# A decode kernel of two layers: 640 columns of ring given to resident W_q, another fill order for the first MLP's ring, no unread products in the first and last norm

## The chip, the cores and the metric

The kernel runs on one core of one Trainium2 chip. The metric is the device time of one execution in microseconds (us). Several executions of each kernel are timed and the median is taken; one more execution is profiled, and every duration below comes from that one.

## The reference

Two layers run one after the other on a single token of each of four sequences (B = 4, D = 640). Both layers use the same weights and the same caches. A layer is an attention over the last 1024 positions of a cache of 32 heads of 128, and then a gated MLP of width 1728; both are added to the residual, and both read a layernorm without weights.

```python
def _A_ref(x, k_cache, v_cache, wq, wo):
    W = min(4096, max(256, Sk // 4))          # 1024
    q = (x @ wq).reshape(B, Sq, Hq, Dh)       # 32 heads of 128, then transposed
    k, v = k_cache[:, :, Sk - W:, :], v_cache[:, :, Sk - W:, :]
    scores = jnp.einsum("bhqd,bhkd->bhqk", q, k) * (Dh ** -0.5)
    p = _softmax(scores, axis=-1)
    o = jnp.einsum("bhqk,bhkd->bhqd", p, v)
    return o.transpose(0, 2, 1, 3).reshape(B, Sq, Hq * Dh) @ wo

def _B_ref(x, W_gate, W_up, W_down):
    gate, up = x @ W_gate, x @ W_up
    return (gate * (gate > 0) * up) @ W_down

x = x + _A_ref(_layernorm(x), ...)
x = x + _B_ref(_layernorm(x), ...)
x = x + _A_ref(_layernorm(x), ...)
x = x + _B_ref(_layernorm(x), ...)
```

Everything is float32. Both layers need all of K and V of the 1024 positions, W_q, W_o and the MLP; they are loaded twice, but for the part that stays on the chip.

## The kernel before

The host lays out all weights and caches as four long arrays of 128 rows, in the order in which the kernel uses them: `heads` (W_q, K, W_o and V of heads 0 to 26, in six groups of four and one of three), `kept` (the same for heads 27 to 31, in groups of three and two), `mlp`, and `limbs` (the last 512 columns of V of head 17, cut into short pieces for a few rows). The two kept groups are K0 and K1 (KEPT = 5 heads): the first layer uses them last, the second layer first, and they stay in memory between.

**The store.** One tile, `store`, of 128 rows x STORE floats holds all that is loaded. A second, `first_q`, of HELD floats keeps the first columns of `heads` (W_q of the first group and a part of the second's) for both layers. HELD + STORE is constant. A list `plan` names every load in order: its array, its columns, and the place in `store` that it is written to. `put` adds loads to it, `stretch` adds a long run of them that goes round `store` as a ring (pieces of at most MOST floats, three to a lap, LAP).

**What sets the order.** `load()` issues loads from the plan on SP, strictly in order, until one whose place still holds data that is to be used (`live`). Each use of data ends in `done`, which frees the columns that were used and calls `load()` again. So each load is issued behind the instruction that uses its place for the last time, and a load that can't be issued holds up all that come after it in the plan. SP does nothing else. This order is fixed when the program is built; on the chip, SP waits on TensorE's semaphore.

**TensorE's order in attention**, for a group g with the group `before` and the group `after`: totals and transposed probabilities of g, `query` of the group after next, `scores(after)` (uses K of the next group), `project(before)` (uses W_o of the group before), `values(g)` (uses V of g). In the first layer the part of `heads` that is used last is thus W_q ..., V of heads 20 to 23, W_o of heads 20 to 23, V of heads 24 to 26, W_o of heads 24 to 26.

**From the heads to the kept part.** In the first layer, `kept` is loaded while the last heads are still being used. The columns of `heads` from `turn` on lie in `store` from 2 * KEPT * D = 6400; `turn` is the first cut (an end of a part that can be used by itself) from which all the rest fits in. Over them `kept` is written in pieces: 6400 to 18688, 18688 to 26880, 26880 to 33536, and five more. The third one's end is written as v0 + 6656.

**The first MLP.** Then 47360 floats (FRONT) of `store` are taken by `kept`. The MLP of the first layer goes through a small ring: the space above FRONT, and three places inside the kept part, AHEAD (768 floats, named `a` in the plan), AWAY (`q`, 1280) and BACK (`k`, 1728), whose data ScalarE copies to `probs` and to PSUM for that time. AWAY's data comes back after down(0). The lists `gu`, `gu_end` and `wd` give the places and sizes of the MLP's loads by hand. `gate(j)` uses the columns of a quarter of W_gate and W_up, in pieces of 256 floats; `down(j)` uses W_down in four pieces of 640, in the order down(3), down(0), down(1), down(2). Behind the MLP's loads come the first loads of the second layer's `heads`, from column HELD on, into the same ring, then a ring that grows as the kept data is used.

**Unread products.** `busy` and `fill` multiply the identity with itself into PSUM, where nobody reads it, when `waits[0]` is set. `normalized` sets it and issues two transposes and one product.

Of the kernel before, what the change touches and what calls it, by code (L numbers as in the profile page):

```python
# [57 lines left out]

HELD = 4288
STORE = 50624
FRONT = KEPT * 2 * (D + KV)


# [1 line left out]
BACK = FRONT - 2 * KV - 1728, FRONT - 2 * KV  # L67
AWAY = BACK[0] - 1280, BACK[0]
HOME = 12864
FIRST, MOST = 32384, 16192  # L70
LAP = 3 * MOST
SPLIT, PART = 17, 2048
LIMBS = [(half + i, 5, 0, 1536) for i in range(4) for half in (0, 32)] + [(i, 2, 1536, PART) for i in range(4)]
# [39 lines left out]
def decode_kernel(ctx: ExitStack, tc: tile.TileContext, x, source, out):  # L113
# [21 lines left out]
    def put(layer, row, to, *cuts):  # L135

        for lo, hi in zip(cuts, cuts[1:]):
            assert 0 < hi - lo <= MOST and to % 64 == 0 and lo % 32 == hi % 32 == 0 and to + hi - lo <= STORE, (row, lo, hi, to)
            plan.append((layer, row, lo, hi, to))
            to += -(-(hi - lo) // 64) * 64  # L140
        return to
# [29 lines left out]
    q_end = 2 * KEPT * D  # L171
    turn = min(c for c in ROWS["heads"][2] if c >= heads_end - (STORE - q_end))
    mid = [near(turn + (heads_end - turn) * i // 3) for i in (1, 2)]
    to = stretch(0, HELD, turn, FIRST)
    assert to <= KEPT * D or to > 2 * MOST, to
    put(0, "kept", KEPT * D, KEPT * D, q_end)
    put(0, "heads", q_end, turn, *mid, heads_end)
# [2 lines left out]


    f, z, a, q, k = FRONT, STORE - D, AHEAD[0], AWAY[0], BACK[0]
    assert STORE - FRONT == 2 * 1280 + 64 + D
    gu = [(z, D), (f, 1280), (f + 1280, 1344), (a, 768), (k, 960), (k + 960, 768), (q, 1280)]
    gu_end = [(f, 1280), (f + 1280, 1280), (f + 2560, D)]
    wd = [(a, D), (k, 960), (k + 960, D), (q, 1280), *gu_end, (a, D), (k, D), (k + D, D)]
    lo = 0
    for to, n in gu + gu + gu_end + wd:
        put(0, "mlp", to, lo, lo + n)
# [2 lines left out]


    lo = HELD
    for to, n in (f, 1280), (f + 1280, 1280), (f + 2560, D + 64), (a, 768), (k, 1728):
        put(1, "heads", to, lo, lo + n)
        lo += n
    to = AHEAD[1]
# [10 lines left out]
    to = put(1, "heads", to, lo, hi)  # L209
    lo, hi = hi, near(hi + STORE - to)  # L210
    put(1, "heads", to, lo, hi)
    last = near(heads_end - 25216)
    to = stretch(1, hi, last, 0)
    for lo, hi in (last, near(last + 12800)), (near(last + 12800), heads_end):
        to = put(1, "heads", to if to + hi - lo <= STORE else 0, lo, hi)
    cuts = [0, 7040, 12160, GU0 + 3 * GU, WD1 + WD, MLP - 4 * D, MLP - 2 * D, MLP - D, MLP - QUARTER, MLP]
    for lo, hi in zip(cuts, cuts[1:]):
# [152 lines left out]
            nc.tensor.matmul(m[32 * g:32 * g + 32], sel_q, a, start=True, stop=True, tile_position=(0, 32 * g))  # L370
        return m

    def normalized():

        ysb, xc, sq = probs[:, :QUARTER], gates[:, :QUARTER], gates[:, QUARTER:2 * QUARTER]
        waits[0] = True
        nc.vector.tensor_reduce(su, y, axis=AX.X, op=ALU.add)
        nc.scalar.copy(ysb, y)
        busy(2)
        mu = mean(su)  # L380
        nc.vector.tensor_tensor(xc, ysb, mu.to_broadcast([P, QUARTER]), op=ALU.subtract)
        nc.scalar.activation(sq, xc, AF.Square, accum_out=ss)
        fill(1)
        nc.vector.transpose(xT, xc)
        return ss
# [140 lines left out]

    def attention(layer):
        gs = order[layer]
        rstd = deviation(normalized())
        table(AF.Exp)  # L530
        query(layer, gs[0], True)
        query_out(gs[0], rstd)
        query(layer, gs[1])
        query_turned(gs[0])
        go_on()
        query_out(gs[1], rstd)
        scores(layer, gs[0])
        query(layer, gs[2])
        softmax(gs[0])
        query_turned(gs[1])  # L540
        query_out(gs[2], rstd)
        for before, g, after, then in zip([None] + gs, gs, gs[1:] + [None], gs[2:] + [None] * 2):
            totals(g)
            turned()
            if layer == 0 and after is None:
                nc.scalar.copy(probs[:, QUARTER:QUARTER + 768], store[:, AHEAD[0]:AHEAD[1]])
                nc.scalar.copy(ps.rearrange("p j n -> p (j n)"), store[:, BACK[0]:BACK[0] + 1024])
                nc.scalar.copy(yy[:, QUARTER:3 * QUARTER], store[:, BACK[1] - 320:BACK[1]])
                free(*AHEAD)
            if before is not None:  # L550
                values_turned(before)
            if then is not None and before is not None:
                query(layer, then)
                query_out(then, rstd)
            if after is not None:
                scores(layer, after)
                softmax(after)
            else:
                table(AF.Sqrt)
            if then is not None:  # L560
                query_turned(then)

            if before is not None and not (layer == 0 and after is None):
                project(layer, before)
            values(layer, g, after is None)
        values_turned(gs[-1])
        if layer == 0:
            for i in range(2):
                nc.scalar.copy(banks[i][:, P:], away[:, 512 + 384 * i:896 + 384 * i])
            free(*AWAY)  # L570
            project(layer, gs[-2])
        fill(1)
        project(layer, gs[-1], True)

    def forward(layer):
        ss = normalized()
        gus, hTs = {}, {}

        def gate(j):
            n, groups = (P, 4) if j < 3 else (64, 3)  # L580
            at = GU0 + j * GU if j < 3 else 0
            gus[j] = pp[:, j % 2, :2 * P]
            for c in range(KC):
                for g in range(groups):
                    lo = at + (c * groups + g) * 2 * n
                    product(gus[j][32 * g:32 * g + 32], xT[:, 32 * c:32 * c + 32], layer, "mlp", lo, 2 * n,
                            start=c == 0, stop=c == KC - 1, tile_position=(0, 32 * g))
                    done(layer, "mlp", lo, 2 * n)

        def gated(j):  # L590
            n, p = (P, P) if j < 3 else (64, 96)
            gu = gus.pop(j)
            at = P * (j + 1) % 512
            a, b = gates[:p, at:at + n], probs[:, :P] if j < 3 else gates[:p, 3 * P:3 * P + n]
            nc.scalar.activation(a, gu[:p, :n], AF.Relu, scale=rstd[:p])
            nc.vector.scalar_tensor_tensor(b, gu[:p, n:2 * n], rstd[:p], a, op0=ALU.mult, op1=ALU.mult)
            return b

        def hidden(j, h):
            if j < 3:  # L600
                hTs[j] = gates[:, P * j:P * j + P].rearrange("p (f x) -> p f x", f=4)[:, :, :B]
                nc.vector.transpose(gates[:, P * j:P * j + P], h)
                return
            hTs[j] = probs[:, P:P + 2 * B].rearrange("p (f x) -> p f x", f=2)
            ph = bank(P).rearrange("p (f x) -> p f x", f=4)
            for g, lo, f in (0, 0, 0), (1, 64, 0), (2, 0, 1), (2, 64, 1):
                nc.tensor.matmul(ph[lo:lo + 64, f, :B], h, ident[:96, 32 * g:32 * g + B],
                                 start=True, stop=True, tile_position=(0, lo))
            nc.vector.tensor_copy(hTs[j], ph[:, :2, :B])

        def down(j, last=False):
            for f in range(4 if j < 3 else 1):
                lo = WD1 + j * WD + f * D if j < 3 else WD0
                for g in range(4):
                    product(y[32 * g:32 * g + B], hTs[j][:, f], layer, "mlp", lo + g * QUARTER, QUARTER,
                            start=False, stop=last and f == 3, tile_position=(0, 32 * g))
                done(layer, "mlp", lo, D)
                if j == 3:
                    fill(1)
                elif not (last and f > 1):  # L620
                    busy(1)
                if j == 0 and f == 1:
                    fill(2)
            if j == 3:
                for g in range(4):
                    r = slice(64 * (g // 2), 64 * (g // 2) + 64)
                    product(y[32 * g:32 * g + B], hTs[j][r, 1], layer, "mlp", TAIL + g % 2 * QUARTER, QUARTER,
                            start=False, stop=False, rows=r, tile_position=(r.start, 32 * g))
                done(layer, "mlp", TAIL, 2 * QUARTER)

        gate(3)
        waits[0] = layer == 0
        rstd = deviation(ss)
        go_on()
        fill(1)
        h = gated(3)
        for j, j1 in (3, 0), (0, 1), (1, 2):
            gate(j1)
            hidden(j, h)
            fill(1)  # L640
            h = gated(j1)
        down(3)
        down(0)
        hidden(2, h)
        if layer == 0:
            nc.scalar.copy(away[:, :512].rearrange("p (j n) -> p j n", j=2), pp[:, :, 256:])
            for i in range(2):
                nc.scalar.copy(away[:, 512 + 384 * i:896 + 384 * i], banks[i][:, P:])
            live[AWAY[0]:AWAY[1]] = [True] * 1280
        down(1)  # L650
        down(2, last=True)
# [62 lines left out]
```

## Time and profile before

| | before |
|---|---|
| median of 3 timed executions | 730.42 us (730.34 to 730.63) |
| profiled execution, its own time | 730.35 us |
| span of its profile, first to last instruction | 728.5 us |
| bytes read from HBM | 310.49 MB |
| DMA packets, in all | 13482 |
| mean rate over the span | 427 GB/s |
| granted TensorE clock, mean | 0.826 |

The span is what the profile divides: engines' busy shares, windows, waits and the chain of work that ended last are all in us from its start. A row of a window gives its length, then the busy time of TensorE (PE), its weight loads (PEld), VectorE, ScalarE and GpSimd, each with the number of instructions, then the granted clock, the share of the time in which the sixteen DMA engines were busy, on average, and the GB/s that they moved. A row of the timeline gives start, length, engine, line, operation, the tiles written and read, and in brackets the idle time of that engine before it and what ended this. All matrix products have line 272, that of `product`, so they are told apart by the tile that they write: `ps` or `pp` for scores, `po` for values, `y` for W_o and W_down, `m` for queries, `pp` for the gates. A float32 product stands as two records.

### The profile page before, as it was taken

The page shows a single profiled execution, that of the slowest core. Times are in us where ns is not written, and L with a number is a line of the kernel's source. Part 1 is how long each engine was busy: PE and PEld are TensorE (multiplying, and loading weights), DVE is VectorE, ACT ScalarE, POOL GpSimd, SP SyncE. Part 2 cuts the span into 40 slices and gives each one's busy share as a digit, 9 for nine tenths or more (in the row PEclk, how much of TensorE's full clock was granted, in tenths as well). Part 3 has the DMA queues.
Part 4 walks back from the last instruction along what each step waited for, and adds up shares of the span by engine and source line. Part 5 has one row for each costly group of instructions (what it writes and reads, how often), then busy time and mean ns, then how long its engine had stood idle before and what let it go on. Part 6 is the DMA issues. An engine that isn't in the chain of part 4 may idle for free.

```text
span 728.5 us, 8337 instructions
## 1 busy us (share of the span) xinstructions
PE 442.4 (61%) x3816; PEld 142.2 (20%) x3816; DVE 70.0 (10%) x215; ACT 54.2 (7%) x101; POOL 1.8 (0%) x11
## 2 busy tenths in 40 slices
PE   3545564644655475519878896465655556557576
PEld 1111111111111121103333241021111112102123
DVE  2010010000010000002111211001000010001011
ACT  2000000000000000001312210000000000000100
POOL 0000000000000000000000000000000000000000
PEclk9978787977778786759999999677777787859889
DMA  9999999999999999999999999999999999999997
GB/s 406 447 394 447 439 444 444 401 441 437 439 432 421 418 456 421 440 423 429 417 413 413 435 429 448 443 430 436 419 440 436 437 436 415 448 435 430 420 423 301
DMA packets 13482, 311.10 MB, mean 427 GB/s; under 512 B 1572, under 2 KB 1956, under 8 KB 7176
## 3 DMA queue, kind: packets, MB, share of 16 engines
q1 hardware_dynamic: 13440, 310.56, 99.2%
q8 instruction: 30, 0.49, 0.2%
q14 instruction: 4, 0.03, 0.0%
q10 hardware_dynamic: 8, 0.01, 0.0%
HBM read 310.49 MB, written 0.08 MB: 426 GB/s over the span
## 4 chain that ended last, share of the span: by engine, by line
DMA 77%; PE 20%; SPq 1%; issue 1%; DVE 0%; ACT 0%; DVEq 0%
DMA store<-in_heads 61%; PE ps L272 9%; DMA store<-in_kept 8%; DMA store<-in_mlp 8%; PE po L272 6%; PE m L272 2%; PE y L272 1%; PE pp L272 1%; PE pp L457 1%; PE m L428 1%; SPq L237 1%; PE po L486 0%; PE m L513 0%; PE m L504 0%; PE y L400 0%
## 5 line engine op out<-in xcount | busy, mean ns | idle before, releaser
L272 PE MATMUL po<-store,pT 128*16 128x512 f32 (+1 forms) x1024 | 155.8, 712 | 125.5 <-DMA store<-in_heads 118.8
L272 PE MATMUL ps<-store,qT 128*4 128x512 f32 (+3 forms) x996 | 147.5, 676 | 102.4 <-DMA store<-in_heads 81.1
L272 PEld LDWEIGHTS po<-store,pT 128*16 128x16 f32 x1024 | 32.1, 109 | 232.4 <-DMA store<-in_heads 122.4
L272 PEld LDWEIGHTS ps<-store,qT 128*4 128x4 f32 x996 | 29.5, 92 | 202.6 <-DMA store<-in_heads 92.0
L453 ACT ACTIVATE probs<-ps,nm 128x1024 f32<-128x1024 f32 x17 | 18.9, 1113 | 332.9 <-DVE nm L449 332.9
L272 PE MATMUL m<-store,xT 128*32 128x512 f32 (+4 forms) x150 | 29.5, 598 | 23.2 <-DMA store<-in_heads 23.2
L449 DVE TENSOR_REDUCE nm<-ps 128x1 f32<-128x1024 f32 x17 | 20.8, 1225 | 230.1 <-PE ps L272 230.1
L272 PE MATMUL y<-store,oT 128*4 128x160 f32 x512 | 22.0, 305 | 11.0 <-DMA store<-in_heads 9.8
L500 ACT COPY gates<-po 128x512 f32<-128x512 f32 x16 | 9.4, 586 | 259.7 <-PE po L272 259.7
L272 PE MATMUL pp<-store,xT 128*32 128x256 f32 (+3 forms) x322 | 20.1, 350 | 8.7 <-DMA store<-in_mlp 4.2
L466 DVE COPY pT<-pp 128x32 f32<-128x32 f32 x64 | 10.3, 185 | 135.9 <-PE po L272 117.3
L457 PE MATMUL pp<-sel_sb,probs 128*128 128x128 f32 x144 | 20.1, 286 | 0.0
L457 PEld LDWEIGHTS pp<-sel_sb,probs 128*128 128x128 f32 x144 | 17.8, 150 | 0.0
L506 DVE RECIPROCAL r<-m 128x16 f32<-128x16 f32 x18 | 4.6, 257 | 132.0 <-PE m L504 132.0
L272 PEld LDWEIGHTS y<-store,oT 128*4 128x4 f32 x512 | 12.3, 87 | 18.8 <-DMA store<-in_heads 10.1
L421 DVE TENSOR_SCALAR gates<-m,rstd 128x512 f32<-128x512 f32 (+2 forms) x18 | 12.4, 689 | 29.2 <-PE m L272 29.2
L272 PEld LDWEIGHTS pp<-store,xT 128*32 128x32 f32 x322 | 10.4, 109 | 17.0 <-DMA store<-in_mlp 7.6
L272 PEld LDWEIGHTS m<-store,xT 128*32 128x32 f32 x150 | 6.3, 116 | 35.7 <-DMA store<-in_heads 25.8
L428 PE MATMUL m<-sel_sb,gates 128*128 128x128 f32 x64 | 12.7, 324 | 0.0
L513 PE MATMUL m<-sel_sb,gates 128*128 128x128 f32 x72 | 11.7, 284 | 0.8 <-DVE gates L493 0.8
L428 PEld LDWEIGHTS m<-sel_sb,gates 128*128 128x128 f32 x64 | 7.9, 160 | 19.6 <-issue 19.1
L272 PE MATMUL y<-store,gates 128*4 128x160 f32 x192 | 9.8, 299 | 2.2 <-DMA store<-in_mlp 2.1
(82 smaller groups left out, 131.5 us busy)
## 6 DMA issues: line engine op xcount, KB each, us to landing
store<-in_heads SPq DMA_DIRECT2D x15, 7936.0 KB
store<-in_heads SPq DMA_DIRECT2D x3, 8096.0 KB
store<-in_heads SPq DMA_DIRECT2D x3, 7872.0 KB
store<-in_heads SPq DMA_DIRECT2D x2, 8032.0 KB
store<-in_heads SPq DMA_DIRECT2D x1, 8000.0 KB
store<-in_heads SPq DMA_DIRECT2D x1, 7424.0 KB
store<-in_heads SPq DMA_DIRECT2D x1, 7360.0 KB
store<-in_heads SPq DMA_DIRECT2D x1, 7168.0 KB
```

Source lines behind the costliest of these rows:

```text
L237: nc.sync.dma_start(out=store[p:p + 4 * n - 3:4, to + a:to + b], in_=source[row][p:p + 4 * n - 3:4, a:b])
L272: nc.tensor.matmul(out[:, a:z], by, t[rows, p:p + z - a], start=start and not a, stop=stop and z == n, **how)
L421: nc.vector.tensor_scalar(gates[:, :len(HEADS[g]) * P], qp.pop(g), rstd, SCALE, op0=ALU.mult, op1=ALU.mult)
L428: nc.tensor.transpose(qt[:, i], gates[:, i * P:(i + 1) * P], ident)
L449: nc.vector.tensor_reduce(nm[g], to.rearrange("p j n -> p (j n)"), axis=AX.X, op=ALU.max, negate=True)
L453: nc.scalar.activation(probs, sc.pop(g).rearrange("p j n -> p (j n)"), AF.Exp, bias=nm.pop(g), accum_out=sums[g])
L457: nc.tensor.transpose(pp[:, c // 4, c % 4 * P:c % 4 * P + P], probs[:, c * P:(c + 1) * P], ident)
L466: nc.vector.tensor_copy(to, pp.rearrange("p j (c x) -> p (j c) x", c=4)[:, :, i:P:32])
L500: nc.scalar.copy(gates, po)
L506: nc.vector.reciprocal(r[g], so.rearrange("p (b i) -> p i b", b=B)[:, :SIDE])
L513: nc.tensor.transpose(ot[:, 127 * b:127 * b + P], gates[:, b * P:(b + 1) * P], ident)
```

## The change

HELD grows from 4288 to 4928 floats and STORE shrinks from 50624 to 49984. The assertion on the size of a load is 16320 now, `stretch` takes pieces of at most 15936 (MOST), and the first store load, of up to 16320, is put by itself. The lists of the first MLP's ring are other ones: 26 loads instead of 27, and the second layer's heads begin with four loads into that ring instead of five. Two constants near the end of the second layer's heads follow. The places from which the kept part is written, v0 + 6656 among them, are not edited. `normalized` takes an argument that says whether unread products are issued: not in the first norm (attention of the first layer) and not in the last (MLP of the second).

```diff
-HELD = 4288
-STORE = 50624
+HELD = 4928
+STORE = 49984
...
-FIRST, MOST = 32384, 16192
+FIRST, MOST = 31872, 15936
...
-            assert 0 < hi - lo <= MOST and to % 64 == 0 and lo % 32 == hi % 32 == 0 and to + hi - lo <= STORE, (row, lo, hi, to)
+            assert 0 < hi - lo <= 16320 and to % 64 == 0 and lo % 32 == hi % 32 == 0 and to + hi - lo <= STORE, (row, lo, hi, to)
...
     turn = min(c for c in ROWS["heads"][2] if c >= heads_end - (STORE - q_end))
     mid = [near(turn + (heads_end - turn) * i // 3) for i in (1, 2)]
-    to = stretch(0, HELD, turn, FIRST)
+    first = near(HELD + 16320)
+    put(0, "heads", FIRST, HELD, first)
+    to = stretch(0, first, turn, 0)
...
     f, z, a, q, k = FRONT, STORE - D, AHEAD[0], AWAY[0], BACK[0]
-    assert STORE - FRONT == 2 * 1280 + 64 + D
-    gu = [(z, D), (f, 1280), (f + 1280, 1344), (a, 768), (k, 960), (k + 960, 768), (q, 1280)]
-    gu_end = [(f, 1280), (f + 1280, 1280), (f + 2560, D)]
-    wd = [(a, D), (k, 960), (k + 960, D), (q, 1280), *gu_end, (a, D), (k, D), (k + D, D)]
+    assert STORE - FRONT == 1280 + 704 + D
+    gu = [(z, D), (f, 1280), (f + 1280, 704), (a, 768), (k, 960), (k + 960, 768), (q, 1280)]
+    gu_end = [(f, 1280), (f + 1280, 1280), (a, 768), (k, 1152)]
+    wd = [(q, 960), (f, 1280), (f + 1280, 1280), (a, D), (k, 1280), (f, 1280), (f + 1280, 1280), (a, D)]
...
     lo = HELD
-    for to, n in (f, 1280), (f + 1280, 1280), (f + 2560, D + 64), (a, 768), (k, 1728):
+    for to, n in (f, 1280), (f + 1280, 1344), (a, 768), (k, 1728):
         put(1, "heads", to, lo, lo + n)
...
-    last = near(heads_end - 25216)
+    last = near(heads_end - 26368)
     to = stretch(1, hi, last, 0)
-    for lo, hi in (last, near(last + 12800)), (near(last + 12800), heads_end):
+    for lo, hi in (last, near(last + 13184)), (near(last + 13184), heads_end):
...
-    def normalized():
+    def normalized(warm):
...
-        waits[0] = True
+        waits[0] = warm
...
-        rstd = deviation(normalized())
+        rstd = deviation(normalized(layer > 0))
...
-        ss = normalized()
+        ss = normalized(layer == 0)
```

## The prediction

> **What bounds the kernel now.** I read the busy shares and the DMA queues first, then the chain of work that ended last, then the stages by windows.
>
> ```profile
> PE 442.4 (61%) x3816; PEld 142.2 (20%) x3816; DVE 70.0 (10%) x215; ACT 54.2 (7%) x101; POOL 1.8 (0%) x11
> q1 hardware_dynamic: 13440, 310.56, 99.2%
> q8 instruction: 30, 0.49, 0.2%
> DMA 77%; PE 20%; SPq 1%; issue 1%; DVE 0%; ACT 0%; DVEq 0%
> 2.00:360.00 358.00, 200.45 (x1541) 59.13 (x1541) 30.55 (x92) 24.16 (x39) 0.50 (x3) 0.81 1.00 432
> 360.00:395.00 35.00, 27.64 (x386) 14.02 (x386) 4.32 (x15) 6.03 (x16) 0.00 (x0) 1.00 1.02 414
> 1.70:720.00 718.30, 438.48 (x3732) 140.26 (x3736) 69.05 (x211) 54.17 (x101) 0.73 (x4) 0.82 1.00 431
> 720.00:724.80 4.80, 3.32 (x84) 1.71 (x74) 0.00 (x0) 0.00 (x0) 0.00 (x0) 1.00 0.70 275
> ```
>
> The loads that SP issues take 99.2% of sixteen DMA engines, TensorE 61% of the span. The last two columns of the windows are the DMA share and GB/s. From 1.70 to 720 us the share is 1.00: on average no engine pauses. So **the kernel is one stream of bytes**, and only three things move its end: fewer bytes, less cost per load, or a moment at which the stream runs dry. The first MLP (360 to 395) streams 414 GB/s against 432 before it. Its loads are small, 25 or so in the window, so (1 - 414/432) x 35 us = 1.46 us, about 0.06 us for each load.
>
> In the last window the share is 0.70, 3.36 of 4.80 us: the average engine is done at 723.36. The chain ends so:
>
> ```profile
> 694.25 30.52 DMA store<-in_mlp
> 724.77 0.04 issue
> 724.81 0.65 PE y L272 x8
> ```
>
> The last landing is seen at 724.77, so the average engine finishes up to 1.41 us ahead of the last. I call this the **lead**. Whole 128-row loads cannot make it, because they give each engine the same work. What can are things that fall on single engines, such as the 30 instruction packets of q8, 16 KB each, and the limb loads of 2 or 5 rows.
>
> **The change part by part.** *Bytes.* W_q columns 4288 to 4928 stay for the second layer. 640 floats x 128 rows x 4 B = 0.328 MB less at 431 GB/s is **-0.76 us**. In the first layer these columns only move from the first store load into first_q, and the total is equal. *Loads.* The first MLP takes 26 for 27 and the head of the second layer 4 for 5; counted through, the other splits differ in size but not in number. Two loads at 0.06 are **-0.12 us**.
>
> *Unread products.* Two transposes and one product go from the first norm and again from the last.
>
> ```profile
> L361 PE MATMUL po<-sel_sb 128*128 128x128 f32 x2 | 0.8, 500 | 0.0
> L354 PE MATMUL po<-sel_sb 128*128 128x128 f32 x2 | 0.7, 448 | 0.0
> 8.29 4.06 PE L272 MATMUL m<-first_q,xT 128*32 128x512 f32 x24 [2.32 <-DMA first_q<-in_heads]
> 27.27 1.92 PE L272 MATMUL m<-store,xT 128*32 128x320 f32 x4 [14.92 <-DMA store<-in_heads]
> ```
>
> They take 1.5 us of TensorE in the first norm, and behind them TensorE waits 2.32 and then 14.92 us for loads. The last norm lies inside the chain's transfer from 694.25 to 724.77. I cost both at **nothing**; without that cover they would give at most 1.5 us each. The longer first_q lands later by the same 0.76 us, in front of the same 14.92 us wait.
>
> *The kept load that moves.* The first layer's heads from column `turn` on lie in the store from 6400. STORE shrinks by 640, so `turn` moves to the next cut, from 211328 to 211840: 512 columns. The split of the kept part keeps its literal v0 + 6656. Its third load fills 26880 to 33536, which before held columns up to 238464, exactly the end of V of head 23. Now it holds 512 columns more, the beginning of W_o of head 20. So this load no longer waits for V of head 23 but for the first head of project(5), which comes after scores(7). SP's issues stay in order, and all later loads stand behind it, first the rest of the kept part, for which TensorE waits now from 338.04 on. Where it stood, and where the new release lies:
>
> ```profile
> 301.42 0.33 SPq L241 DMA_DIRECT2D store<-in_kept  x1
> 325.11 0.04 issue
> 325.16 6.78 PE ps L272 x48
> 332.24 1.27 PE L272 MATMUL y<-store,oT 128*4 128x160 f32 x32
> 338.04 20.08 DMA store<-in_kept
> L272 PE MATMUL y<-store,oT x56: 298/299/300, 332.2 to 344.5; 128*4 128x160 f32 x56
> store<-in_kept SPq DMA_DIRECT2D x1, 4096.0 KB
> ```
>
> It was issued at 301.42, with work ahead of it until 334.82 (below). Scores(7) wait for the kept load before last, whose landing is seen at 325.11. The first of four heads in project(5) is 8 of 32 records: the eighth starts near 332.24 + 7 x 0.031 = 332.46, lasts 0.30 and ends near 332.76, and SP issues 0.06 later, at **332.82**. Only one load is then still under way, 4096 KB behind the one seen at 325.11: 4.194 MB / 432 GB/s = 9.71 us, seen at 334.82. Is 2.0 us enough? What a start from an empty queue costs is shown twice:
>
> ```profile
> 0.73 0.38 SPq L228 DMA_DIRECT2D first_q<-in_heads  x1
> first_q<-in_heads SPq DMA_DIRECT2D x1, 2144.0 KB
> store<-in_heads SPq DMA_DIRECT2D x3, 8096.0 KB
> 725.87 0.35 SPq L657 DMA_DIRECT2D out_x<-probs  x1
> SPq L709 <- DMA out_x<-probs: 1.2, 1, 1.2
> out_x<-probs SPq DMA_DIRECT2D x1, 80.0 KB
> ```
>
> The first two loads, 10.49 MB or 24.27 us, were issued from 0.73 and seen at 27.27 less 0.04: 2.23 us of start and notice. The output is issued at 725.87, takes 0.35 to issue and is awaited 1.2 us more; less 0.19 for its bytes that is 1.36. I take **2.23**, the row of a full load from HBM, and keep 1.36 as the low end. Then the stream resumes at 335.05 against 334.82: the last engine pauses 0.23 us, and every leading engine loses its lead. With 1.36 the last engine has 0.62 us to spare.
>
> *The shorter ring.* Before, the first MLP ends on pieces at f, f+1280, f+2560, a, k, k+640. Now they are k (1280), f, f+1280, a (640), and then the second layer's first load wants f again, which is free after down(2,0). When the last piece that this needs has landed, only f+1280 and a are under way: 1920 floats, 0.983 MB, **2.37 us** at 414 GB/s. Before, the same load had 3840 floats, 4.75 us. From landing to issue, this is the row of the same step now (two pieces of 640 in a load, and the issue behind them):
>
> ```profile
> 390.18 0.45 PE L272 MATMUL y<-store,gates 128*4 128x160 f32 x8 [0.28 <-DMA store<-in_mlp]
> 390.82 0.46 PE L272 MATMUL y<-store,gates 128*4 128x160 f32 x8
> 391.34 0.33 SPq L241 DMA_DIRECT2D store<-in_heads  x1
> ```
>
> That is 391.34 - 390.18 + 0.04 = 1.20 us. With the start it needs 1.20 + 2.23 = 3.43 us. Before there were 4.75, so 1.32 to spare, about the average lead, which is why the share stayed near 1. Now there are 2.37: **the last engine pauses 1.06 us** (0.19 with the low start cost), and the others their lead besides. The next load, for f+1280, has the same distance and finds the time just paid for. The two loads before have 3200 floats, 3.96 us, and some 0.5 to spare. Earlier in the MLP 2880 floats or more stand against a release that comes after the first gate block of a piece, and the pause of the first place is not repeated there.
>
> *The lead.* At a dry place all engines resume together. That costs the end nothing if those that led have no more single work to come; it costs the whole lead if the end again stands 1.41 us above the average, because new single work falls anywhere. From nothing to 2 x 1.41; I take one lead, **1.41**, because the second place comes 60 us after the first and finds a part of the spread rebuilt.
>
> **Sum** against the profiled execution (728.5 span, 730.35 with what lies around it; the median of the three times is 730.42): -0.76 - 0.12 + 0.23 + 1.06 + 1.41 = **+1.82**, on the median **732.2 us**.
>
> **The rivals.**
>
> 1. *The queue never runs dry.* The start cost is nearer to 1.36 (the output's row), and a load issued 2 us ahead is ready in time. For it: the share of 1.00 and 1.02 over all of before. Against it: the 2.23 of the first load. Result: -0.88 + 0.19, **729.7**. This is the case that is not slower; it decides where start and notice fall below 2.37 - 1.20 = 1.17 to 2.0 us.
> The Trainium skill, DMA: Bandwidth & Descriptors, section "Latency and other measured facts", gives about 0.6 us to the first byte of a DMA from SP. By that rule both places stay fed (0.6 is less than 2.0 and less than 1.17), which is this rival's case and would give 729.5. The first load's row speaks against it, 2.23 us, though that row has the notice in it.
>
> 2. *Dry for the last engine alone*: the pauses come, the leads count for nothing. -0.88 + 1.29 = +0.41, **730.8**.
>
> 3. *Further dry places*: the two loads with 0.5 us to spare fall short also and both leads are lost. 1.29 + 2.82 + 0.5 - 0.88 = +3.7, **734.1**.
>
> 4. *The change doesn't do what it says*: the columns are loaded again after all. The second layer's plan begins at HELD, so I give this no chance of its own.
>
> **How the numbers follow.** Forecast 0.50 (its own range 731.5 to 733.2), rival 1 0.17, rival 2 0.20, rival 3 0.13. A measurement tells about 0.2% from no change, 1.46 us: faster is below 728.96, slower above 731.88. Faster by that much would need more than the bytes: 0.02. Slower: rival 3 and most of the forecast, 0.56. Within: rivals 1 and 2 and the forecast's lower edge, 0.42. The range that leaves out the lower part of rival 1 and the upper of rival 3 is 730.0 to 733.7.
>
> **What would show it.** The third kept load, 3328 KB, is issued near 332.8 and not near 301; the waits of SP have a release by `y` there. The DMA share of a window around 331 to 336 falls below 1, and so it does around 390 to 396, where the first load of the second layer's heads is issued with two small loads ahead. All later steps are late by 1 to 3 us. I am wrong if those windows stay at 1.00 or above, or if they fall and the end still comes at 729.7. HBM read must be 0.33 MB less, and SP must issue two loads fewer.

## The result and the profile after

| | before | after |
|---|---|---|
| median of 5 timed executions, us | 730.34 (730.19 to 730.63) | 738.46 (737.16 to 740.48) |
| ratio, 95% interval | | 1.0114 [1.0102, 1.0125] |
| profiled execution, its own time / span, us | 730.35 / 728.5 | 739.47 / 737.6 |

The change costs 8.1 us, not the 1.8 of the forecast, and the executions spread over 3.3 us where those of before spread over 0.4. The page of the kernel after: busy shares, the queue of the loads (packets, MB, share of sixteen DMA engines), bytes, and the chain of work that ended last.

```profile
PE 450.6 (61%) x3816; PEld 148.7 (20%) x3816; DVE 70.1 (9%) x215; ACT 54.2 (7%) x101; POOL 1.8 (0%) x11
...
q1 hardware_dynamic: 13152, 310.24, 98.5%
...
HBM read 310.16 MB, written 0.08 MB: 421 GB/s over the span
...
DMA 72%; PE 25%; DVE 1%; issue 1%; SPq 1%; ACT 1%; DVEq 0%
```

The 0.33 MB are gone as intended (310.49 before), and yet the stream ends later: 421 GB/s over the span for 426, and TensorE has 25% of the chain for 20%. So it paused, and the windows show where. The last three columns are the granted clock, the DMA share and GB/s. First the kernel before:

```profile
331.00:336.00 5.00, 5.00 (x70) 1.68 (x65) 1.71 (x5) 1.21 (x2) 0.00 (x0) 1.00 0.93 401
...
380.00:390.00 10.00, 8.02 (x108) 3.98 (x108) 0.98 (x3) 1.28 (x3) 0.00 (x0) 1.00 1.02 416
390.00:400.00 10.00, 8.77 (x125) 3.99 (x129) 2.25 (x7) 3.00 (x8) 0.00 (x0) 1.00 1.03 410
400.00:410.00 10.00, 8.97 (x77) 2.91 (x73) 2.45 (x5) 2.93 (x5) 0.00 (x0) 1.00 1.03 425
410.00:425.00 15.00, 13.94 (x135) 5.57 (x131) 3.15 (x9) 1.79 (x3) 0.00 (x0) 1.00 1.04 445
```

The same windows after:

```profile
331.00:336.00 5.00, 5.00 (x70) 1.61 (x62) 1.52 (x4) 1.20 (x2) 0.00 (x0) 1.00 0.61 210
...
380.00:390.00 10.00, 7.71 (x84) 3.86 (x84) 1.32 (x4) 1.20 (x3) 0.00 (x0) 0.83 0.99 362
390.00:400.00 10.00, 7.10 (x98) 2.84 (x93) 0.00 (x0) 0.98 (x3) 0.00 (x0) 0.94 0.91 320
400.00:410.00 10.00, 9.75 (x88) 4.31 (x84) 2.37 (x7) 2.47 (x6) 0.00 (x0) 0.55 0.92 323
410.00:425.00 15.00, 12.90 (x110) 3.94 (x106) 3.88 (x8) 4.13 (x7) 0.00 (x0) 1.00 1.02 420
```

A shortfall in GB/s times the length of the window is the bytes that were not moved; over 431 GB/s it is lost time. At 331 to 336 that is (401 - 210) x 5 / 431 = 2.2 us. From 380 to 410 it is 1.25 + 2.1 + 2.4 = 5.7 us, from 410 to 425 0.9. Together 8.8 (over all of 320 to 440, where 422 GB/s became 391, it is 8.6). Less the 0.9 that the forecast gives for bytes and loads saved, this is 7.9 of the 9.1 us between the two profiled executions. Two places were forecast, 331 to 336 and 390 to 396. **The second is three windows wide**, and its last one lies mostly behind the MLP, at 0.55 of TensorE's clock.

The chain of work around that place in the kernel before (start, us, what):

```profile
394.84 0.04 issue
394.88 0.50 PE y L272 x8
...
397.32 1.68 PE m L272 x26
...
399.79 5.33 PE pp L272 x48
```

The chain around the same place after:

```profile
394.00 5.73 DMA store<-in_mlp
399.73 0.04 issue
399.77 0.72 PE y L274 x8
...
400.90 1.18 PE y L274 x16
...
404.17 3.33 PE m L274 x26
...
408.88 3.19 PE pp L274 x25
```

From the last MLP landing that TensorE waits for to the scores of the second layer's first group it takes 4.9 us before and 9.1 after. This is not all the same work: before, one part of W_down is still to be used behind that landing, after, three. From the end of the last W_down product it is 399.79 - 395.38 = 4.4 us before and 408.88 - 402.08 = 6.8 after. The same 26 products of the first queries take 1.68 us and 3.33, which is most of this difference. The loads of the second layer wait for the places that this chain frees, so a slow TensorE now holds up the stream.

The end of the profiled execution after is TensorE's as well: where the chain of before ended in a 30.52 us transfer and one block of `y`, the chain of after ends without a wait for a load.

```profile
723.18 4.01 PE pp L274 x40
...
728.03 2.37 PE pp L274 x40
730.39 4.10 PE y L274 x112
```

Two gate blocks of the same 40 records stand there with 4.01 and 2.37 us. From 720 to 737.6 the loads still move 272 GB/s on average, where before moved 80 in a window as long: (272 - 80) x 17.6 / 431 = 7.8 us by which the stream is late. The other 1.3 of the 9.1 us lie behind it, at TensorE.

### The profile page after: what moved, and what is told of

Its sections match the earlier page's. It is cut to its first block, busy times and chain, and to the rows that moved or that the text cites. A ratio compares the mean times of both kernels' runs of the same rounds, so it can differ in the third digit from the quotient of the medians.

```text
span 737.6 us, 8332 instructions
## 1 busy us (share of the span) xinstructions
PE 450.6 (61%) x3816; PEld 148.7 (20%) x3816; DVE 70.1 (9%) x215; ACT 54.2 (7%) x101; POOL 1.8 (0%) x11
## 4 chain that ended last, share of the span: by engine, by line
DMA 72%; PE 25%; DVE 1%; issue 1%; SPq 1%; ACT 1%; DVEq 0%
DMA store<-in_heads 60%; PE ps L274 9%; DMA store<-in_kept 8%; PE po L274 7%; DMA store<-in_mlp 4%; PE pp L274 3%; PE y L274 2%; PE m L274 2%; PE pp L459 1%; PE m L430 1%; SPq L239 1%; PE po L488 1%; PE m L515 0%; PE po L356 0%; PE m L506 0%
## 5 line engine op out<-in xcount | busy, mean ns | idle before, releaser
L274 PE MATMUL po<-store,pT 128*16 128x512 f32 (+2 forms) x1028 | 152.2, 695 | 132.0 <-DMA store<-in_heads 124.5
L274 PE MATMUL ps<-store,qT 128*4 128x512 f32 (+2 forms) x996 | 154.0, 693 | 106.4 <-DMA store<-in_heads 83.9
L274 PEld LDWEIGHTS ps<-store,qT 128*4 128x4 f32 x996 | 31.1, 94 | 211.6 <-DMA store<-in_heads 95.1
L274 PE MATMUL m<-store,xT 128*32 128x512 f32 (+4 forms) x146 | 27.9, 601 | 20.9 <-DMA store<-in_heads 20.9
L274 PE MATMUL pp<-store,xT 128*32 128x256 f32 (+2 forms) x326 | 25.8, 430 | 8.2 <-DMA store<-in_mlp 4.2
L274 PEld LDWEIGHTS pp<-store,xT 128*32 128x32 f32 x326 | 12.8, 132 | 18.6 <-DMA store<-in_mlp 7.3
```

The lines of the kernel that those rows point to most:

```text
L274: nc.tensor.matmul(out[:, a:z], by, t[rows, p:p + z - a], start=start and not a, stop=stop and z == n, **how)
```

## The experiments

Each was timed in 5 rounds beside the kernel before, whose median stayed between 730.27 and 730.45 us. "Cut" is the end of the third kept load, v0 + 6656 in both kernels.

| run | edit | median (range), us | ratio to before, 95% |
|---|---|---|---|
| e6_before_norms | before, norms of the change | 730.30 (730.21 to 730.53) | 1.0000 [0.9991, 1.0010] |
| e4_norms | after, all unread products back | 738.66 (734.50 to 739.44) | 1.0107 [1.0091, 1.0124] |
| e7_before_split | before, cut 512 later | 733.15 (732.34 to 733.59) | 1.0038 [1.0024, 1.0051] |
| e1_split | after, cut 512 earlier | 735.38 (733.25 to 736.38) | 1.0065 [1.0053, 1.0077] |
| e2_order | after, other order of the heads' loads | 736.51 (734.52 to 741.59) | 1.0097 [1.0073, 1.0121] |
| e3_split_order | e1 and e2 | 736.47 (734.84 to 737.59) | 1.0086 [1.0073, 1.0099] |
| e10_warm_gates | e3, unread transposes in the gates | 738.57 (737.31 to 739.82) | 1.0119 [1.0103, 1.0135] |
| e9_ring | e1, ring cut finer | 733.42 (732.22 to 733.91) | 1.0040 [1.0027, 1.0053] |
| e11_before_ring | before, short ring alone | 734.91 (733.90 to 736.60) | 1.0062 [1.0050, 1.0074] |
| e12_before_fine | before, short ring cut finer | 734.61 (731.81 to 735.41) | 1.0049 [1.0037, 1.0061] |
| e13_before_fine_warm | e12, five unread transposes | 731.36 (730.81 to 733.90) | 1.0019 [1.0010, 1.0028] |
| e14_ring_warm | e9, five unread transposes | 731.69 (731.05 to 733.80) | 1.0024 [1.0015, 1.0032] |
| e15_split_warm | e1, twelve unread transposes | 733.36 (732.69 to 735.94) | 1.0049 [1.0036, 1.0061] |

**The unread products.** In the kernel before, the edit to the norms alone:

```diff
-        rstd = deviation(normalized())
+        rstd = deviation(normalized(layer > 0))
...
-        ss = normalized()
+        ss = normalized(layer == 0)
```

> The kernel before with the changed norms alone: no unread products in the first and the last norm, ring and resident columns as before. Theory A (the loads run dry, the ring is too short): the end is still that of the load stream, 730.3 us (730.1 to 731.2). Rival B (the products that went keep TensorE's clock up, and the loads wait for TensorE): 732 or more.

And the opposite edit in the kernel after (`normalized(True)` in both places):

> The changed kernel with the unread products of the first and the last norm back, and nothing else. Theory A: only the tail behind the last load gets shorter, by about 1 us (the changed kernel's 4.7 us from the last landing to the end become 3.8): 737.5 us (736.5 to 738.5). Rival B: most of the 8 us come back, 731 to 733.

Neither changes the time: 1.0000, and 738.66 for 738.46. In a kernel whose loads are on time the unread products are worth nothing. In the kernel after, the 1 us that was expected from their return did not come, but its executions spread over 4.9 us (734.50 to 739.44), so a part in the last 1.3 us is neither shown nor excluded.

**The kept load.** In the kernel before, the third kept load alone is made to wait for W_o of head 20:

```diff
-    put(0, "kept", k0, k0, k1, v0, v0 + 6656, v1, v1 + KV, v1 + 7168, FRONT)
+    put(0, "kept", k0, k0, k1, v0, v0 + 7168, v1, v1 + KV, v1 + 7168, FRONT)
```

> The kernel before with one number edited: the third kept load ends at v0 + 7168, so that its place holds W_o of head 20 and it waits for project(5) as in the changed kernel. Nothing of the ring is touched. Theory A: one dry place at 331 to 336 us and no other: 733 us (732 to 734.5). Theory C (a dry place costs the end little as long as the ring behind it has its old length, since only engines that lead are held up): 730.3 to 731.5. Rival B: 730.3.

In the kernel after it is spared that wait:

```diff
-    put(0, "kept", k0, k0, k1, v0, v0 + 6656, v1, v1 + KV, v1 + 7168, FRONT)
+    put(0, "kept", k0, k0, k1, v0, v0 + 6144, v1, v1 + KV, v1 + 7168, FRONT)
```

> The changed kernel (738.5 us) with one number edited: the third kept load ends at v0 + 6144, so that it waits for V of head 23 again. Theory A (two dry places in the load stream make nearly all of the loss): the dry place at 331 to 336 us is gone, the ring's stays: 735.5 us (734.5 to 736.5), and the DMA share of 331 to 336 us is back above 0.9. Rival B (TensorE's lower clock, from the unread products that went, makes the loss, and loads are late only because TensorE is): 738 or more, since no product comes back. If the two dry places overlap in their cost (the second absorbs the engines' idle time of the first): under 1 us, 737.5 to 738.5.

Both hit: +2.9 us alone, -3.1 when taken back. This is the window of e7 at that place:

```profile
331.00:336.00 5.00, 5.00 (x70) 1.60 (x62) 1.52 (x4) 1.20 (x2) 0.00 (x0) 1.00 0.64 223
```

And this is SP's issue of the load in the timeline of e7 (start, us, what):

```profile
334.03 0.33 SPq L241 DMA_DIRECT2D store<-in_kept  x1
```

The issue was forecast at 332.82. Why is it 1.2 us later? TensorE's timeline shows it. First the run with the unread products back, e4:

```profile
325.31 6.69 PE L274 MATMUL ps<-store,qT 128*4 128x512 f32 x48 [22.14 <-DMA store<-in_kept]
```

SP's timeline of e4 has the issue of the load here:

```profile
332.81 3.02 SPq L243 DMA_DIRECT2D store<-in_kept  x2
```

TensorE's timeline of the kernel after:

```profile
325.22 7.94 PE L274 MATMUL ps<-store,qT 128*4 128x512 f32 x48 [22.55 <-DMA store<-in_kept]
```

And SP's:

```profile
333.97 0.33 SPq L243 DMA_DIRECT2D store<-in_kept  x1
```

Scores(7) begin at the same time, after 22 us of idle TensorE, and the same 48 records take 6.69 us in one execution and 7.94 in the other. Where they take 6.69, the load is issued at 332.81. (This is the fastest execution of e4, 734.50 us; the other five lie from 738.54 to 739.44.) The 15 profiled executions of this study have this block between 6.63 and 8.16 us, at mean clocks from 0.64 to 0.50 in the window 320 to 331. The Trainium skill, TensorE: Matmul & The Clock Gate, "Part 1: The HAM clock gate", says that an idle array runs at half clock for about 3.4 us, decided in a free-running window, so that the number of slow products differs from run to run. The 1.5 us of scatter at this place agree. At full clock the same 48 records take 5.33 us (`pp`, in the chain of before above), so by an estimate they ran at half clock for 2 x (6.63 - 5.33) = 2.6 to 2 x (8.16 - 5.33) = 5.7 us, at times longer than the page says.

Is an issue at 332.81, as forecast, early enough? The window of e4, and then of e2 (below), whose load was issued at 333.28:

```profile
331.00:336.00 5.00, 5.00 (x70) 1.73 (x66) 1.71 (x5) 1.21 (x2) 0.00 (x0) 1.00 0.80 295
331.00:336.00 5.00, 5.00 (x70) 1.74 (x66) 1.51 (x4) 1.21 (x2) 0.00 (x0) 1.00 0.71 254
```

It is not. With the issue at 332.81 the window moves 295 GB/s, at 333.28 254, at 333.97 (after) 210 and at 334.03 (e7) 223; in all runs in which the load does not wait for project(5) it moves 400 to 419. At the forecast time (401 - 295) x 5 / 431 = 1.2 us are lost by the average engine, and 2.1 to 2.2 at the real one.

**The order of the second layer's first loads.** The first of them wants `f`, with 1920 floats under way; `k` is free earlier:

```diff
-    for to, n in (f, 1280), (f + 1280, 1344), (a, 768), (k, 1728):
+    for to, n in (k, 1728), (f, 1280), (f + 1280, 1344), (a, 768):
```

> The changed kernel with the four loads that begin the second layer's heads in another order: the place k, free after down(1,2), first, then f, f + 1280, a. 3200 floats are under way at the first of them instead of 1920. Theory A: the dry place near 400 us goes, the one at 331 to 336 stays: 734.5 us (733.5 to 736). Rival B: 738 or more.

With the earlier cut as well:

> Both edits. Theory A: no dry place is left; the 0.88 us of bytes and loads are gained against the kernel before, and about 1 us is lost at the end, where TensorE runs at a lower clock without the last norm's unread products: 730.5 us (729.8 to 731.5), and about 8 us less than the changed kernel. Rival B: 737 or more.

The first can't be told clearly from no effect (738.46 to 736.51, intervals overlap), the second missed by 6 us and is no better than e1. From the last W_down loads on, no load has fewer than 3200 floats ahead (one earlier load of the ring has 2880), and still the stream runs dry. Taking away the 1920 floats that the forecast gives as the cause gains nothing clear. Windows of e3:

```profile
380.00:390.00 10.00, 7.66 (x87) 3.68 (x88) 1.19 (x4) 1.81 (x4) 0.00 (x0) 0.83 0.99 391
390.00:400.00 10.00, 8.49 (x104) 3.39 (x104) 0.32 (x1) 0.29 (x1) 0.00 (x0) 0.83 0.90 306
```

**Only the clock?** E3's gate blocks ran in part at half clock (0.83 from 380 to 390, above). So an unread transpose behind each group of three or four pieces of the first layer's gates:

```diff
                             start=c == 0, stop=c == KC - 1, tile_position=(0, 32 * g))
                     done(layer, "mlp", lo, 2 * n)
+                if layer == 0:
+                    busy(1)
```

> e3_split_order (736.5 us) with one unread transpose more behind every five or fewer pieces of a gate block in the first MLP, twenty in all, so that TensorE is busier between its waits. Theory A: the granted clock of 380 to 400 us rises from 0.83 to about 1, releases come up to 1 us earlier in each lap, and the distance of 3200 floats stays: 735 us (734 to 736.5). Rival B: the clock is the cause, 731 to 732.

Both theories missed: it is 2.1 us slower than e3, at full clock from 370 to 390, as the windows of e10 show:

```profile
370.00:380.00 10.00, 9.38 (x111) 5.08 (x111) 0.92 (x4) 0.37 (x1) 0.00 (x0) 1.00 0.97 347
380.00:390.00 10.00, 8.46 (x91) 3.59 (x91) 1.33 (x4) 1.84 (x5) 0.00 (x0) 1.00 0.99 364
```

The transposes stand between a landing and the next release, and 370 to 380 falls to 347 GB/s, where e3 moves 410. This does not end the theory of the clock. It says only that work on that path costs more than the clock brings there.

**A finer ring.** The short ring of e1, cut so that 3776 floats or more are under way at every load:

```diff
-    gu_end = [(f, 1280), (f + 1280, 1280), (a, 768), (k, 1152)]
-    wd = [(q, 960), (f, 1280), (f + 1280, 1280), (a, D), (k, 1280), (f, 1280), (f + 1280, 1280), (a, D)]
+    gu_end = [(f, 1280), (f + 1280, 1344), (a, 768), (k, 960), (k + 960, 768), (q, 960)]
+    four = [(f + D * i, D) for i in range(4)]
+    wd = [*four, (a, D), (k, D), (k + D, D), *four]
...
-    for to, n in (f, 1280), (f + 1280, 1344), (a, 768), (k, 1728):
+    for to, n in (a, 768), (k, D), (k + D, 1088), (f, D), (f + D, D), (f + 1280, 1344):
```

> The changed kernel with the third kept load ending at v0 + 6144 and with another filling of the same shorter ring: q is used until down(0), f is cut into four pieces of 640 in the last two laps, and the second layer's heads begin in a and k. At least 3776 floats are under way at every release of the first MLP and behind it, where the two edits of e3_split_order left 3200 and the changed kernel 1920. Theory A (the distance at a release decides): 730.0 us (729.6 to 730.8): 0.76 less for the bytes, 0.3 more for five loads more than the changed kernel has. Theory D (a ring that is 640 floats shorter runs dry in whatever order it is filled): 732 or more. Rival B: 735.

Theory D was right on the time. (The run has seven loads more than the kernel after, not five: by 0.06 us each, some 0.4 us.) The windows of e9:

```profile
390.00:400.00 10.00, 8.21 (x107) 3.32 (x104) 1.16 (x4) 1.68 (x5) 0.00 (x0) 0.86 1.02 389
400.00:410.00 10.00, 10.00 (x84) 3.43 (x77) 2.08 (x4) 2.51 (x5) 0.00 (x0) 0.80 0.89 304
```

The MLP is nearly fed; what is left is lost behind it, from 400 on. Two causes were possible: the 640 floats that the second layer no longer has ahead there, or the clock.

**The ring alone, with the 640 floats given back.** The kernel before, with the ring shortened as in the change (its `gu`, `gu_end` and `wd`) and the room used for one more load behind the second layer's first ones:

```diff
-    for to, n in (f, 1280), (f + 1280, 1280), (f + 2560, D + 64), (a, 768), (k, 1728):
+    for to, n in (f, 1280), (f + 1280, 1344), (a, 768), (k, 1728), (z, D):
```

> The kernel before with the ring of the first MLP 640 floats shorter, in the changed kernel's pieces, and nothing else: W_q, the bytes and the third kept load stay, and the 640 floats that the ring gives up are filled by one more load behind the second layer's first five, so that 5,760 floats of them are still asked for ahead of the norm. Theory A (the ring loses its time inside the MLP, in the short laps of 1,920 and 3,200 floats ahead): the split kernel lost 5.1 us against before with 0.8 us of bytes saved, so about 736 us here, 735 to 737, with a lower rate from 385 us on. Theory B (much of the loss is the 640 floats that are missing behind the norm, as the re-cut ring's dry place at 400 to 410 us suggests): 731.5 to 733.5, and full from 400 us on. Prediction as on record (one pause of about 1 us and part of the lead): 731 to 732.5.

And the same with the lists of e9:

> The same with the finer pieces of the re-cut ring (at least 3,776 floats ahead everywhere) in place of the changed kernel's. The bytes are those of before, 0.8 us more than in the re-cut changed kernel (733.4 us). Theory A (what is left in the re-cut kernel is lost behind the norm, where 5,120 floats stand ahead and not 5,760): the place behind the norm is full again, so 730 to 731.5. Theory B (the 640 floats are missing inside the MLP too, however they are cut): 733 to 734.5, with the share of the DMA below 0.95 between 380 and 400 us.

The first came to 734.9, just below the range of theory A: the ring alone costs 4.6 us. The second missed theory A by 3 us and came to the time of B, but not as B has it: its share is 1.03 before 400 and falls only after it. The 640 floats are there, so their absence is not the cause. The windows of e12:

```profile
390.00:400.00 10.00, 7.78 (x99) 3.19 (x99) 0.99 (x3) 0.96 (x4) 0.00 (x0) 0.84 1.03 393
400.00:410.00 10.00, 9.97 (x87) 3.51 (x80) 1.92 (x5) 3.23 (x6) 0.00 (x0) 0.82 0.89 295
```

Its chain behind the MLP:

```profile
399.63 3.33 PE m L273 x26
```

The 26 query products take 3.33 us again.

**The clock in idle time.** Now the unread transposes stand where TensorE would be idle anyway, in the last down step, ahead of the parts that wait for a load:

```diff
                 lo = WD1 + j * WD + f * D if j < 3 else WD0
+                if last and layer == 0 and f > 1:
+                    busy(4 if f == 2 else 1)
```

> The kernel before with the finely cut short ring, which came to 734.6 us, and four unread transposes ahead of the third part of the first layer's last down step and one ahead of its fourth, where TensorE stood idle for 1.42 and 0.32 us waiting for loads. Theory A (what is left of the loss is the clock at the norm: the 20 products of the first query after it took 2.86 us there and 1.50 us before, and the chain from the last down product to the next block of scores 7.3 us and 4.9 us): the clock stays up, the place from 400 to 410 us is full again, 731 to 732.5. Theory B (the loads land late and the clock only follows): no change, 734 to 735, whatever the clock is.

In the changed kernel with the finer ring:

> The same five unread transposes in the changed kernel with the earlier cut and the finely cut ring, which came to 733.4 us. Theory A (the clock at the norm): 730.5 to 731.5, with more than 0.95 of the DMA's time used from 400 to 410 us. Theory B (late loads): 733 to 734.

E13 is 3.3 us faster than e12 by the medians and 2.2 by the ratios, whose intervals are apart; e14 is 1.7 faster than e9 (1.2 by the ratios), with intervals that just overlap, and lies 0.2 above the range of theory A. The window of e13 behind the MLP:

```profile
400.00:410.00 10.00, 8.94 (x73) 3.02 (x71) 2.97 (x7) 3.37 (x7) 0.00 (x0) 1.00 1.03 410
```

Its chain there:

```profile
398.54 1.68 PE m L273 x26
```

The queries are back at 1.68 us, and the stream is full. Last, the ring of the change itself:

```diff
                 lo = WD1 + j * WD + f * D if j < 3 else WD0
+                if layer == 0 and (j, f) in ((0, 0), (1, 3), (2, 1)):
+                    busy(2 + j * 2)
```

> The changed kernel with the earlier cut (735.4 us), its ring as it is, and two, four and six unread transposes in the first layer ahead of the down products that stood idle 0.72, 1.01 and 1.90 us for their loads. From its last waited-for down product to the next block of scores it took 8.1 us, where the kernel before took 4.9. Theory A (the short ring costs most of its 5.1 us through the clock at the norm that follows): the chain goes back towards 4.9 us, so about 3 us less, 731.5 to 733. Theory B (the ring's own laps cost most, and the clock is the smaller part): 733.5 to 735, with the lower rate between 380 and 400 us as it was.

The time lies between the two theories, and the lower rate that theory B names is still there up to 400. The windows of e15:

```profile
390.00:400.00 10.00, 8.05 (x120) 4.04 (x117) 1.12 (x4) 1.13 (x5) 0.00 (x0) 1.00 0.87 281
400.00:410.00 10.00, 9.28 (x87) 2.89 (x79) 3.13 (x7) 4.27 (x7) 0.00 (x0) 1.00 1.02 423
```

2.0 us less than e1 by the medians, 1.2 by the ratios, whose intervals overlap. From 400 on the stream is full again. From 390 to 400 it is still dry, at 281 GB/s with the clock at 1.00: (410 - 281) x 10 / 431 = 3.0 us that the clock does not explain.

## Why the prediction was right or wrong

**Right:** the bytes (0.33 MB less), the two loads fewer, the unread products at nothing (as far as e6 and e4 tell), the first dry place with its cause, and a second one near 390. The direction follows from these. Of the second place the cause named, 1920 floats ahead, is not shown: e2 and e3 remove it and gain nothing that stands clear of the noise. **Wrong:** the size, 8.1 us for 1.8. The runs divide it like this:

| step | forecast, us | measured, us |
|---|---|---|
| bytes and two loads | -0.88 | not timed alone; 0.33 MB less read |
| unread products | 0 | 0.0 (e6); +0.2 when put back (e4) |
| kept load: pause and a lead | 0.23 + 1.41 | +2.9 (e7) |
| shorter ring | 1.06 | +4.6 alone (e11); about +6.0 if the 0.9 is saved (e1 lies 5.1 above before) |
| sum | +1.82 | 2.9 (e7) + 5.1 (e1) = 8.0, for 8.1 |

The forecast counts one lead for both places; it stands here with the first. No run times the 0.9 us by themselves, and e1 and e11, with and without the saving (e11 also has the 640 floats back behind the MLP), have nearly the same ratio to before, 1.0065 and 1.0062. So whether it is gained at all stays open, and the ring's price lies between 4.6 and 6.0 us.

*The kept load that moves.* The mechanism was right; mis-sized was its issue. "Scores(7)" was taken from one execution, 6.78 us, near the quick end of a block that takes up to 8.16. With the issue of e7, 334.03, the prediction's own working gives 334.03 + 2.23 - 334.82 = 1.44 for the pause and 1.41 for the lead: 2.85 for 2.9. That the two terms are each right is not shown by this, only their sum. (The 0.62 us to spare in the low case should read 2.00 - 1.36 = 0.64; nothing hangs on it.)

*The shorter ring* is where the prediction failed: it let the last engine pause once, 1.06 us, gave the two loads before "some 0.5 to spare", let the next one find "the time just paid for", and counted the durations of TensorE as they stood. In e3 3200 floats are not enough, with TensorE at 0.83 of its clock. E9 and e12 show that from 3776 on the MLP stays nearly fed up to 400 us. E15 indicates the shares: about 3 us in the loads' own laps, at full clock, and 1.2 to 2.0 us through TensorE (the intervals of e1 and e15 overlap; those of e12 and e13, where the same step is 2.2 to 3.3 us, do not). This second share the prediction did not consider. Starved of loads, TensorE comes out of the MLP at a lower clock, needs 6.8 us for 4.4 from its last W_down product to the next scores, and so makes the next dry place itself. How the 3 us divide between single laps and leads stays open.

*The rivals.* Rival 1, a queue that never runs dry, is out: in e4 the load is issued at 332.81, the 2.0 us before the queue's end that this rival counts on, and the share still fell to 0.80 and the rate to 295 GB/s; after, with some 0.8 us, to 0.61 and 210. By the 0.6 us to the first byte that the Trainium skill gives (DMA: Bandwidth & Descriptors, "Latency and other measured facts") that place would have stayed fed; these traces disagree, though none shows the first byte itself. Rival 2 is out by the size. Rival 3, further dry places (734.1), named the right thing and was still 4 us short: it has neither the late issue of the kept load nor the slower TensorE.

No version was faster than the kernel before. Of those with the short ring the nearest, e13 and e14, lie 1.0 and 1.4 us above it. The windows of e14 show a part of the reason:

```profile
390.00:400.00 10.00, 8.85 (x126) 4.23 (x126) 1.77 (x5) 2.47 (x6) 0.00 (x0) 1.00 1.02 396
400.00:410.00 10.00, 8.94 (x77) 3.01 (x79) 2.93 (x6) 2.93 (x5) 0.00 (x0) 1.00 1.02 396
```

The kernel before moves 410 and 425 GB/s there: (14 + 29) x 10 / 431 = 1.0 us lost. That alone would be made up by the 0.9 us of the forecast, of which no run shows a gain clear of the noise; where the rest goes is not located.

## What to carry to other kernels

A stream of loads fed through a ring is a loop: landing, use, release, issue, start. When the ring is cut, work out that loop for every load and not only for the shortest, with room for the slowest duration of the using engine rather than that of one execution, since here a place that ran dry also slowed the engine that had to free the next one. A constant in a hand-written plan (v0 + 6656 here) that was fitted to another length is part of the change even where the diff does not touch it.

## What the runs showed of the hardware

TensorE's clock fell without a long idle time: in e12 TensorE is busy for 7.78 of the 10 us from 390 to 400, and the clock there is still 0.84 and then 0.82. This is its longest idle time from 385 to 412, 1.42 us:

```profile
396.04 0.46 PE L273 MATMUL y<-store,gates 128*4 128x160 f32 x8 [1.42 <-DMA store<-in_mlp]
```

The Trainium skill, TensorE: Matmul & The Clock Gate, "Part 1: The HAM clock gate", names an idle window of about 3.4 us for the half clock, and also tells of a kernel whose short idle times between groups of products made the clock swing. No gap of 3.4 us stands here, so the trace is of the second kind. Five unread transposes put into the gaps brought it back to 1.00 from 390 on (e13) and the time down by 3.3 us (2.2 by the ratios); the same means on the path of the loads (e10) cost 2 us. And a block of work behind a long idle time, the same in every execution, took anything from 6.63 to 8.16 us.
